# Two-batch hashed attention with two gated products behind it: a new order of the attention's work, a start with other buffers, and the first weights converted one pair later

## The chip, the cores and the metric

The kernel runs on one core of one Trainium2 chip. The metric is the device time of one execution in microseconds (us), the median of three runs. A core has five engines with queues of their own: TensorE (PE; PEld is its weight load), VectorE (DVE), ScalarE (ACT), GpSimd (POOL) and SyncE (SP, which here only issues DMAs). Each works through its own list in order and waits at semaphores for the others.

## The reference

Attention over 2 batches of 8 heads with 768 positions of width 64, where a query may only look at keys of its own hash bucket, then two products through wider layers:

```python
q_bits = (np.einsum('bhsd,dk->bhsk', q, proj) > 0)      # 6 bits a position; k likewise
mask = q_bucket[:, :, :, None] == k_bucket[:, :, None, :]
scores = np.where(mask, scale * q @ k.T, -1e9)
attn = softmax(scores); x = (attn @ v)                  # 1536 rows of 512
x = (sigmoid(x @ w_gate) * (x @ w_val)) @ w_out         # 512 -> 1536 -> 512
h = x @ w_in                                            # 512 -> 2048
g = h where h >= 1, 0 where h <= -1, else (h + 1) ** 2 / 4
out = g @ w_out2                                        # 2048 -> 512
```

The five weight matrices come as 64-bit floats. A chunk of 128 x 512 is brought to 32 bits on the chip and split into a high and a low part, and a product of two such numbers takes three matmuls.

## The kernel before

**Pairs and units.** Two heads make a pair; there are 8 pairs. A pair has 12 units, a unit being 128 queries of one head against all 768 keys. For each unit: `QK` (4 matmuls: two add the mask by one-hot rows, two the scores), `MAX` (the row maximum, DVE, L305), `EXP` (ACT, L309). Two units of the two heads make a Flip: `T` transposes 4 blocks of 128 x 128 (PE, L329), `HI` writes them to half precision (ACT, L338), `LO` the remainder (DVE, L341); there are 18 of each in a pair. `PV` multiplies with v (PE, L380) in three parts for each third of the queries, `EV` (L387) scales the result into X; `ST`, `RB`, `R` and `RS` turn the sums of the exponentials into row factors. The PSUM tiles are few: two `sc` tiles for scores, two `pt` tiles for transposes, one `mm`, one `pv`.

**Preparation of the next pair** (class `Prep`) runs beside this. q and k are loaded (`load_qk`), scaled and split into U (high) and W (low) by `scale`, `top`, `rest` on GpSimd. `z` projects them on PE, `bits` takes signs on ACT, `xp` multiplies the signs with the table of codes, `H` makes the one-hot rows of it on ACT. `copy` moves half tiles across partitions by DMA on SP's queue: N<-U, U<-W, W<-N, N<-H, H<-U.

**What sets the order.** A table `AT` (L463) gives each kind of operation its place, counted in units from the start of its pair; a place may be negative or beyond 12, and then lies in the pair before or behind. All operations of all pairs are sorted by place (L598) and issued in that order, so the table alone sets how each engine's list reads. Nothing is scheduled at run time.

**The start.** The first pair has no pair before it. Its split runs on ACT and DVE (`UW`), its tiles are moved by `first_moves` and `swap` on SP (L246, L259), its products with the codes are held in two `sc` tiles (`xp`, L452 to L460). 12 matmuls on a tile of zeros run ahead (`idle`, L434). The first chunk of `w_gate` is loaded between the q and k of pair 0 and of pair 1 (L432), that of `w_val` behind v (L450). Both are converted by `first_weights`, whose steps stand at places -1.25 to 4.75 of pair 0 (L590); its tiles are taken from the tags PT and P of the attention.

**The end of the attention and the rest.** `gv(0)` (L597), the first half of the first gate and value products, stands behind the last transposes; its DVE product (L154) is issued with it. Then come the gate and value products, `out1`, and `mlp2`, which ends with one evacuation and one DMA for each 128 rows (L678).

Of the kernel before, what the change touches and what calls it, by code (L numbers as in the profile page):

```python
# [27 lines left out]
def lsh_attention_glu_act(ctx, tc, qt, kt, v, proj, w_gate, w_val, w_out1, w_in2, w_out2, ident_d, code_d, out):  # L28
# [115 lines left out]

    X = {}

    def gate_val_n(b, n, ws, hr, bank, sgt, nm):
# [6 lines left out]
        nc.vector.scalar_tensor_tensor(out=hr[:, n * HN:(n + 1) * HN], in0=sg, scalar=1.0, in1=pv, op0=ALU.add, op1=ALU.mult)  # L154

    with ExitStack() as actx:
        ap = actx.enter_context(tc.tile_pool(name="attn", bufs=2))
# [22 lines left out]
        class Prep:  # L180
# [67 lines left out]
            def first_copies(self):
                tU, tW, tH, tN, tB = self.t4[0]
                for dst, src in ((tN[O], tU[O]), (tH[E], tU[E])):  # L250
                    nc.scalar.activation(out=dst, in_=f(src), func=AF.Copy)
# [145 lines left out]
        with tc.manual_schedule():  # L397
            ws0, wraw = [], []

            def load_w(w, t):  # L400
# [50 lines left out]
            pp.bits()
            hold = []  # L452
            for j in range(2):
                pp.xp(j)
                hold.append(pp.x_ps)
            for dst, r in ((2, O), (3, E)):
                pp.x_ps = hold[0]
                pp.Hot(0, pp.t4[0][dst], r)
                pp.x_ps = hold[1]
                pp.Hot_k(pp.t4[1][dst], r)  # L460
            pp.done()
            next(fw)
            AT = {  # L463
                "QK": (-2.69, -2.15, -0.16, -0.04, 1.61, 3.54, 3.80, 5.03, 6.14, 7.33, 8.42, 8.60),
                "MAX": (-2.19, -0.38, 0.24, 1.43, 3.32, 4.18, 4.48, 5.61, 6.44, 8.18, 8.87, 9.62),
                "EXP": (-0.83, -0.27, 0.55, 2.99, 3.75, 4.59, 5.42, 6.75, 8.09, 8.26, 8.91, 9.66),
# [13 lines left out]
                "TOP": (-3.20, -1.20),  # L480
                "RST": (-2.90, -0.90),
                "V2": (1.65,),
                "V3": (2.65,),
                "V4": (4.65,),
                "RB": (3.00, 8.00, 10.83),
                "VR": (9.72,),
                "VT": (11.80,),
# [39 lines left out]
            def split_x(b, c):  # L527
# [10 lines left out]
            for q in range(NQ):
                us = un[UP * q:UP * q + UP]
# [224 lines left out]
```

## Time and profile before

| what | us |
|---|---|
| median of 3 runs (lowest, highest) | 830.96 (830.45, 831.16) |
| profiled execution | 829.85 |
| its span (first to last instruction) | 827.8 |
| busy: PE | 805.3 |
| busy: DVE | 550.4 |
| busy: ACT | 457.3 |
| busy: POOL | 117.8 |

The profile is one execution. A busy time is the union of an engine's instructions; of PE the ends are modelled, so that a busy PE can still lose time between matmuls. Instructions of one engine overlap a little: one may start before the one ahead has ended, so a step is read from start to start. Attention takes the first 259 us, the products the rest.

### The profile page before, as it was taken

To read this page: it belongs to the slowest core of one execution; us is meant where nothing else is said; L and a number is where in the kernel's file an instruction comes from. 1 tells how busy PE (TensorE), PEld (TensorE's weight loads), DVE (VectorE), ACT (ScalarE), POOL (GpSimd) and SP (SyncE) were. 2 spreads that over 40 slices of the span, in tenths; PEclk is the share of its full clock that TensorE was granted. 3 is DMA by queue.
4 is the path that set the end of the run, shared out by engine and by line. 5 is a ranking of instruction groups with operands and counts; after the bars stand their busy time and mean duration, and the time that the engine had idled before them with its cause. 6 is when DMAs were issued, how large, how long until landed. Compare 5 with 4: busy or idle time off the path is not lost.

```text
span 827.8 us, 13043 instructions
## 1 busy us (share of the span) xinstructions
PE 805.3 (97%) x5084; PEld 735.8 (89%) x5084; DVE 550.4 (66%) x976; ACT 457.3 (55%) x870; POOL 117.8 (14%) x103
## 2 busy tenths in 40 slices
PE   6799999999998999999999999999999999999997
PEld 4688888888778999999999999999899999999996
DVE  4999898989993754345489767999944435344443
ACT  4788888888882422223233435557655455545453
POOL 4263445435073000000000000000000000000000
PEclk7999999999999999999999999999999999999999
DMA  7443544443201413211245320453200001000001
GB/s 230 115 95 99 134 107 96 125 125 68 59 1 62 144 51 94 60 51 52 89 165 179 96 82 27 152 175 126 81 1 1 1 0 77 1 1 1 1 0 77
DMA packets 39581, 64.21 MB, mean 78 GB/s; under 512 B 5316, under 2 KB 27972, under 8 KB 39520
## 3 DMA queue, kind: packets, MB, share of 16 engines
q1 hardware_dynamic: 39168, 63.20, 26.4%
q8 instruction: 40, 0.66, 0.3%
q14 instruction: 21, 0.17, 0.1%
q0 software_dynamic: 48, 0.11, 0.0%
q10 hardware_dynamic: 304, 0.07, 0.0%
HBM read 45.27 MB, written 3.15 MB: 58 GB/s over the span
## 4 chain that ended last, share of the span: by engine, by line
PE 80%; DVE 10%; DMA 6%; ACT 2%; issue 2%; SPq 0%; DVEq 0%; ACTq 0%
PE sc L297 7%; PE pt L329 7%; PE O L380 6%; PE o L676 5%; PE o L677 5%; PE o L675 5%; PE p L128 4%; PE p L130 4%; PE p L129 4%; PE pg L130 4%; PE pv L129 4%; PE pv L130 4%; PE pg L128 4%; PE pv L128 4%; PE pg L129 4%; PE y L129 2%
## 5 line engine op out<-in xcount | busy, mean ns | idle before, releaser
L341 DVE SCALAR_TENSOR_TENSOR PT<-pt,PT 128x512 f16<-128x512 f32 x144 | 96.4, 685 | 10.7 <-ACT PT L338 7.5
L305 DVE TENSOR_REDUCE st<-sc 128x1 f32<-128x768 f32 x96 | 90.9, 947 | 9.4 <-PE sc L297 9.3
L338 ACT ACTIVATE PT<-pt 128x512 f16<-128x512 f32 x144 | 82.1, 596 | 22.6 <-PE pt L329 21.4
L309 ACT ACTIVATE P<-sc,st 128x768 f32<-128x768 f32 x96 | 86.9, 905 | 13.5 <-DVE st L305 13.2
L329 PE MATMUL pt<-ident,P 128*128 128x128 f32 x576 | 83.2, 279 | 4.5 <-DVE PT L341 3.8
L128 PE MATMUL p<-yh,wh_i 128*128 128x384 f32 x256 | 86.1, 336 | 0.4 <-DVE yl L632 0.3
L130 PE MATMUL p<-yh,wl_i 128*128 128x384 f32 x256 | 85.9, 336 | 0.0
L129 PE MATMUL p<-yl,wh_i 128*128 128x384 f32 x256 | 85.7, 335 | 0.0
L329 PEld LDWEIGHTS pt<-ident,P 128*128 128x128 f32 x576 | 66.2, 142 | 18.5 <-DVE PT L341 11.5
L677 PE MATMUL o<-wh_o,gl 128*128 128x512 f32 x192 | 75.3, 392 | 0.0
L676 PE MATMUL o<-wl_o,gh 128*128 128x512 f32 x192 | 75.2, 392 | 0.0
L675 PE MATMUL o<-wh_o,gh 128*128 128x512 f32 x192 | 74.7, 389 | 0.0
L659 DVE SCALAR_TENSOR_TENSOR g<-p,t 128x384 f32<-128x384 f32 x64 | 35.5, 555 | 48.3 <-ACT t L657 48.3
L154 DVE SCALAR_TENSOR_TENSOR h<-sg,pv 128x384 f32<-128x384 f32 x48 | 26.4, 550 | 53.9 <-PE pv L130 53.9
L660 ACT ACTIVATE gh<-g 128x384 fp32r<-128x384 f32 x64 | 33.6, 525 | 43.7 <-DVE g L659 43.5
L152 ACT ACTIVATE sg<-pg 128x384 f32<-128x384 f32 x48 | 23.4, 487 | 62.1 <-PE pg L130 61.6
L656 ACT ACTIVATE t<-p,cst 128x384 f32<-128x384 f32 x64 | 36.6, 573 | 36.8 <-PE p L130 36.8
L380 PE MATMUL O<-PT,vh 128*64 128x256 f16 x576 | 54.9, 278 | 1.7 <-DVE xr L387 1.7
L661 DVE TENSOR_TENSOR gl<-g,gh 128x384 fp32r<-128x384 f32 x64 | 35.7, 558 | 31.5 <-ACT gh L660 31.5
L128 PEld LDWEIGHTS p<-yh,wh_i 128*128 128x128 f32 x256 | 48.1, 188 | 2.4 <-DVE g L659 0.7
L129 PEld LDWEIGHTS p<-yl,wh_i 128*128 128x128 f32 x256 | 48.1, 188 | 1.1
L118 DVE TENSOR_TENSOR wl_o<-w_o,wh_o 128x512 fp32r<-128x512 f32 x56 | 38.6, 689 | 14.7 <-ACT wh_o L117 14.7
(258 smaller groups left out, 2015.6 us busy)
## 6 DMA issues: line engine op xcount, KB each, us to landing
wr_o<-in_moe_w_out_dram SPq DMA_DIRECT2D x28, 512.0 KB, 3.5
wr_i<-in_moe_w_in_dram SPq DMA_DIRECT2D x16, 512.0 KB, 3.8
wr_g<-in_moe_w_gate_dram SPq DMA_DIRECT2D x12, 512.0 KB, 3.6
wr_v<-in_moe_w_val_dram SPq DMA_DIRECT2D x12, 512.0 KB, 4.0
n<-in_qt_dram SPq DMA_DIRECT2D x8, 384.0 KB, 3.7
n<-in_kt_dram SPq DMA_DIRECT2D x8, 384.0 KB, 4.3
U<-W SPq DMA_DIRECT2D x16, 192.0 KB, 2.5
vr<-in_v_dram SPq DMA_DIRECT2D x8, 384.0 KB, 3.5
```

The source lines that it names most:

```text
L128: nc.tensor.matmul(ps, lhsT=wh, rhs=rh, start=first, stop=False)
L129: nc.tensor.matmul(ps, lhsT=wh, rhs=rl, start=False, stop=False)
L130: nc.tensor.matmul(ps, lhsT=wl, rhs=rh, start=False, stop=last)
L305: nc.vector.tensor_reduce(out=self.st[:, 0, self.c:self.c + 1], in_=self.sc[:, :, 0:HN], op=ALU.max, axis=AX.XY, negate=True)
L309: nc.scalar.activation(out=self.P, in_=self.sc[:, :, 0:HN], func=AF.Exp, bias=self.st[:, 0, self.c:self.c + 1], scale=1.0, accum_out=self. ...
L329: nc.tensor.transpose(self.ps[m][:, j, :], un[2 * self.n + e].P[:, a, c:c + 128], ident)
L338: nc.scalar.activation(out=self.part(0, m), in_=self.ps[m], func=AF.Copy, scale=PSCALE)
L341: nc.vector.scalar_tensor_tensor(out=self.part(1, m), in0=self.ps[m], scalar=PSCALE, in1=self.part(0, m), op0=ALU.mult, op1=ALU.subtract)
L380: nc.tensor.matmul(O_ps[r, 0:GN], lhsT=vv[m][:, e, i * D:(i + 1) * D], rhs=PT[:, l, e * NI + i, :], start=(s == 0), stop=(s == len(steps) ...
L675: nc.tensor.matmul(oacc[i], lhsT=gh[:, ts], rhs=wh, start=(fc == 0), stop=False)
L676: nc.tensor.matmul(oacc[i], lhsT=gh[:, ts], rhs=wl, start=False, stop=False)
L677: nc.tensor.matmul(oacc[i], lhsT=gl[:, ts], rhs=wh, start=False, stop=(fc == F2 - 1))
```

## The change

The table `AT` is replaced by another; its entries for GpSimd (SCL, TOP, RST, V2 to V4, RB) are now numbers of their own, too. Two lines of it:

```diff
-                "QK": (-2.69, -2.15, -0.16, -0.04, 1.61, 3.54, 3.80, 5.03, 6.14, 7.33, 8.42, 8.60),
+                "QK": (-1.70, 0.05, 0.37, 1.03, 1.87, 2.98, 4.26, 5.03, 5.80, 8.96, 9.44, 7.84),
-                "SCL": (-3.80,),
+                "SCL": (-2.94,),
```

The start, the first weights, the held product and the last rows:

```diff
-        nc.scalar.dma_start(proj_sb[E], proj)
-        nc.scalar.dma_start(proj_sb[O], proj)
+        nc.scalar.dma_start(proj_sb, proj)
...
-                raw = ap.tile([128, 2 * S], I64, tag="PT", bufs=3, name=f"wr_{t}_0")[:, 0:512]
+                raw = ap.tile([128, 512], I64, tag="wr", name=f"wr_{t}_0")
...
-                        wt = ap.tile([128, S], U32, tag="P", bufs=7, name=f"w_{t}_0")[:, 0:512]
+                        wt = ap.tile([128, 512], U32, tag="wt", name=f"w_{t}_0")
...
-            load_w(w_gate, "g")
             load_qk(*seq[1], nc.sync)
             idle = sc_tile("idle")
-            for i in range(12):
+            for i in range(26):
...
+            pp.first_copy(nc.gpsimd.tensor_copy, 0)
             p1.scale()
...
-            pp.first_copies()
+            pp.first_copy(nc.scalar.copy, 1)
             pp.z(0, 12)
             for j in range(2):
                 pp.swap(j)
+            pp.bits()
+            xq = sc_tile("xq")
+            xk = [pA.tile([128, 512], F32, tag="pt", bufs=PTB, name=f"xk_{n}")[:, 0:HN] for n in range(2)]
+            for j in range(2):
+                for a in range(2):
+                    nc.tensor.matmul(xk[a] if j else xq[:, a, 0:HN], lhsT=code[:, a, j, :], rhs=bt, start=True, stop=True)
...
+            pp.rest_copies()
+            pp.done()
             load_v(*seq[0], nc.sync)
+            load_w(w_gate, "g")
             load_w(w_val, "v")
...
-            for i in range(7):
-                at(i - 1.25, 0, 0, next, fw, None)
+            for i in range(10):
+                at(2.0 * i, 0, 1, next, fw, None)
...
+            at(max(AT["LO"] + AT["EV"][1:2]) + 0.01, 0, last, lambda: late.pop()())
...
+            if b == B - 1 and i == NI - 1:
+                for eng, h, fn in ((nc.sync, 0, nc.vector.tensor_copy), (nc.scalar, 1, nc.scalar.copy)):
+                    cs = slice(h * DM // 2, (h + 1) * DM // 2)
+                    fn(ob[:, 1, cs], oacc[i][:, cs])
+                    eng.dma_start(rows[:, i, cs], ob[:, 1, cs])
+                continue
```

`proj` is now laid twice under itself by the host, so that one DMA fills both halves. The two copies of B (`rest_copies`) stand behind the one-hot rows instead of ahead of `z`. `first_weights` has ten steps instead of eight; the first ran ahead of the table and now all ten stand in it, in pair 1 and the first half of pair 2. `gate_val_n` takes a list and, for `gv(0)`, puts its DVE product there, to be issued behind the last LO and the second EV.

Three places, as the built programs list them. First SP's list from the loads of pair 0 on; n are q and k, wr_g and wr_v the raw weight chunks, B, N, H, U and W tiles of the pair. Before:

```order
L166 DMA n_0_0_78<-in_kt_dram 128x768
L402 DMA wr_g_96<-in_moe_w_gate_dram 128x4x128
L166 DMA n_0_1_98<-in_qt_dram 128x768
L166 DMA n_0_1_100<-in_kt_dram 128x768
L246 DMA B_133<-U_0_0_115 64x768
L246 DMA N_0_0_122<-U_0_0_119 64x768
L246 DMA B_137<-U_0_0_119 64x768
L246 DMA H_0_0_121<-U_0_0_119 64x768
L259 DMA U_0_0_115<-W_0_0_116 64x768
L259 DMA U_0_0_119<-W_0_0_120 64x768
L172 DMA vr_0_165<-in_v_dram 128x2x384
L402 DMA wr_v_167<-in_moe_w_val_dram 128x4x128
```

The same stretch of SP's list in the changed program:

```order
L171 DMA n_0_0_78<-in_kt_dram 128x768
L171 DMA n_0_1_94<-in_qt_dram 128x768
L171 DMA n_0_1_96<-in_kt_dram 128x768
L251 DMA B_143<-U_0_0_125 64x768
L251 DMA N_0_0_132<-U_0_0_129 64x768
L251 DMA B_148<-U_0_0_129 64x768
L251 DMA H_0_0_131<-U_0_0_129 64x768
L266 DMA U_0_0_125<-W_0_0_126 64x768
L266 DMA U_0_0_129<-W_0_0_130 64x768
L177 DMA vr_0_190<-in_v_dram 128x2x384
L406 DMA wr_g_192<-in_moe_w_gate_dram 128x4x128
L406 DMA wr_v_194<-in_moe_w_val_dram 128x4x128
```

The load of the first gate chunk has moved from ahead of pair 1's q and k to behind v.

Second, DVE's list from the last third of pair 0 to the first MAX of pair 1 (xr is EV's result, vm the maximum over v, sc the scores). Before:

```order
L315 RECIPROCAL st_0_0_2_291<-st_0_0_2_291 128x4
L341 SCALAR_TENSOR_TENSOR PT_0_1_360<-pt_0_411,PT_0_1_360 128x4x128
L305 TENSOR_REDUCE st_0_0_4_405<-sc_0_1_4_417 128x1
L341 SCALAR_TENSOR_TENSOR PT_0_1_360<-pt_2_439,PT_0_1_360 128x4x128
L305 TENSOR_REDUCE st_0_0_4_405<-sc_0_0_5_469 128x1
L341 SCALAR_TENSOR_TENSOR PT_0_1_360<-pt_1_452,PT_0_1_360 128x4x128
L387 SCALAR_TENSOR_TENSOR xr_0_510<-O_0_0_375,rs_0_1_1_393 128x256
L305 TENSOR_REDUCE st_0_0_4_405<-sc_0_1_5_486 128x1
L341 SCALAR_TENSOR_TENSOR PT_0_2_517<-pt_0_498,PT_0_2_517 128x4x128
L341 SCALAR_TENSOR_TENSOR PT_0_2_517<-pt_1_505,PT_0_2_517 128x4x128
L349 TENSOR_REDUCE vm_1_538<-vr_1_391 128x1
L305 TENSOR_REDUCE st_1_0_0_545<-sc_1_0_0_512 128x1
```

The same stretch of DVE's list in the changed program:

```order
L345 SCALAR_TENSOR_TENSOR PT_0_1_328<-pt_2_371,PT_0_1_328 128x4x128
L309 TENSOR_REDUCE st_0_0_4_395<-sc_0_1_5_390 128x1
L345 SCALAR_TENSOR_TENSOR PT_0_1_328<-pt_0_403,PT_0_1_328 128x4x128
L353 TENSOR_REDUCE vm_1_454<-vr_1_368 128x1
L345 SCALAR_TENSOR_TENSOR PT_0_1_328<-pt_1_413,PT_0_1_328 128x4x128
L309 TENSOR_REDUCE st_0_0_4_395<-sc_0_1_4_418 128x1
L345 SCALAR_TENSOR_TENSOR PT_0_2_469<-pt_0_464,PT_0_2_469 128x4x128
L309 TENSOR_REDUCE st_0_0_4_395<-sc_0_0_5_458 128x1
L345 SCALAR_TENSOR_TENSOR PT_0_1_328<-pt_2_475,PT_0_1_328 128x4x128
L391 SCALAR_TENSOR_TENSOR xr_0_519<-O_0_0_423,rs_0_1_1_398 128x256
L309 TENSOR_REDUCE st_1_0_0_528<-sc_1_0_0_511 128x1
```

The last unit's MAX now comes ahead of the two before it, and the first MAX of pair 1 stands behind EV with one LO fewer ahead of it.

Third, DVE's list at the end of the attention, around the product of `gv(0)` (L154, h<-sg,pv). Before:

```order
L341 SCALAR_TENSOR_TENSOR PT_3_2_3526<-pt_0_3561,PT_3_2_3526 128x4x128
L341 SCALAR_TENSOR_TENSOR PT_3_2_3526<-pt_1_3609,PT_3_2_3526 128x4x128
L154 SCALAR_TENSOR_TENSOR h_0_3623<-sg_0_0_3637,pv_0_0_3639 128x384
L341 SCALAR_TENSOR_TENSOR PT_3_2_3526<-pt_2_3616,PT_3_2_3526 128x4x128
L387 SCALAR_TENSOR_TENSOR xr_3_3524<-O_3_1_3528,rs_3_1_3_3550 128x256
L387 SCALAR_TENSOR_TENSOR xr_3_3524<-O_3_2_3655,rs_3_1_5_3671 128x256
```

The same stretch of DVE's list in the changed program:

```order
L345 SCALAR_TENSOR_TENSOR PT_3_2_3500<-pt_1_3584,PT_3_2_3500 128x4x128
L316 TENSOR_SCALAR st_3_0_4_3439<-st_3_0_4_3439,vm_3_3093 128x4
L319 RECIPROCAL st_3_0_4_3439<-st_3_0_4_3439 128x4
L345 SCALAR_TENSOR_TENSOR PT_3_2_3500<-pt_2_3604,PT_3_2_3500 128x4x128
L391 SCALAR_TENSOR_TENSOR xr_3_3546<-O_3_1_3565,rs_3_1_3_3553 128x256
L154 SCALAR_TENSOR_TENSOR h_0_3625<-sg_0_0_3639,pv_0_0_3641 128x384
L391 SCALAR_TENSOR_TENSOR xr_3_3546<-O_3_2_3676,rs_3_1_5_3660 128x256
```

The product has moved behind the last LO and the second EV.

## Rows read from the trace of the kernel before

**Rows 1.** Stretch, length, busy us of PE, PEld, DVE, ACT, POOL; PE clock, DMA, GB/s
```profile
0.00:17.40 17.40, 10.29 (x33) 5.85 (x34) 7.01 (x17) 7.58 (x9) 8.58 (x11) 0.81 0.79 232
17.40:48.80 31.40, 26.64 (x175) 21.48 (x175) 29.19 (x48) 23.03 (x48) 11.36 (x10) 0.89 0.45 118
...
77.30:105.80 28.50, 28.39 (x252) 23.64 (x251) 25.55 (x45) 24.50 (x51) 13.18 (x11) 1.00 0.45 112
...
219.80:259.00 39.20, 36.05 (x334) 30.04 (x334) 28.97 (x53) 25.27 (x52) 24.41 (x21) 1.00 0.01 1
...
822.60:827.80 5.20, 0.01 (x1) 0.00 (x0) 0.06 (x1) 0.60 (x1) 0.00 (x0) 0.88 0.53 206
```
**Rows 2.** Timeline: first MAX of pairs 0, 1 and 7 (start, duration, engine, line)
```profile
17.43 0.96 DVE L305 TENSOR_REDUCE st<-sc 128x1 f32<-128x768 f32 x1 [2.74 <-PE sc L297]
...
48.77 0.95 DVE L305 TENSOR_REDUCE st<-sc 128x1 f32<-128x768 f32 x1
...
219.77 0.95 DVE L305 TENSOR_REDUCE st<-sc 128x1 f32<-128x768 f32 x1
```
**Rows 3.** Timeline of the start: loads landing, the swaps, the first scores
```profile
4.40 0.84 ACT L200 ACTIVATE U<-n 128x768 fp32r<-128x768 f32 x1 [0.53 <-DMA n<-in_qt_dram]
...
5.62 0.84 ACT L200 ACTIVATE U<-n 128x768 fp32r<-128x768 f32 x1 [0.37 <-DMA n<-in_kt_dram]
...
12.67 1.30 SPq L259 DMA_DIRECT2D U<-W  x2
...
16.41 0.98 PE L297 MATMUL sc<-U,U 128*128 128x384 f32 x2 [1.11 <-DMA U<-W]
```
**Rows 4.** Waits of SP's queue: total us, times, longest
```profile
SPq L259 <- DMA B<-U: 4.4, 2, 4.2
```
**Rows 5.** Groups by line: two of the conversion's steps (busy us, mean ns)
```profile
L102 DVE SCALAR_TENSOR_TENSOR w_g<-wr_g,w_g 128x512 uint32<-128x512 uint32 x12 | 8.3, 691 | 0.4
...
L99 DVE TENSOR_SCALAR w_g<-w_g 128x512 uint32<-128x512 uint32 x12 | 5.1, 421 | 0.1
```
**Rows 6.** Timeline: a conversion step beside GpSimd in pair 0
```profile
26.00 2.33 POOL L361 TENSOR_SCALAR vr<-vr,vm 128x768 f32<-128x768 f32 x1 [8.33 <-DMA vm<-vrow]
...
26.30 1.01 DVE L99 TENSOR_SCALAR w_v<-w_v 128x512 uint32<-128x512 uint32 x1
```
**Rows 7.** Timeline of pair 3: steps of PE and DVE
```profile
118.00 1.04 PE L329 MATMUL pt<-ident,P 128*128 128x128 f32 x8
...
118.79 0.59 PE L297 MATMUL sc<-H,H 128*128 128x384 f32 x2
...
119.27 1.29 DVE L341 SCALAR_TENSOR_TENSOR PT<-pt,PT 128x512 f16<-128x512 f32 x2
...
119.57 0.34 PE L228 MATMUL xp<-bt,code 128*128 128x384 bf16 x1
...
120.47 0.95 DVE L305 TENSOR_REDUCE st<-sc 128x1 f32<-128x768 f32 x1
...
121.34 0.41 DVE L387 SCALAR_TENSOR_TENSOR xr<-O,rs 128x256 f32<-128x256 f32 x1
...
129.40 0.85 PE L380 MATMUL O<-PT,vh 128*64 128x256 f16 x12
```
**Rows 8.** Timeline of pair 3: last H, its second DMA, next pair's first product
```profile
126.21 0.59 ACT L235 ACTIVATE H<-xp,cst 128x384 fp32r<-128x384 f32 x1
...
129.34 0.46 SPq L275 DMA_DIRECT2D H<-U  x1
...
131.99 0.41 PE L297 MATMUL sc<-H,H 128*128 128x384 f32 x1
```
**Rows 9.** Timeline of the hand-over: PE behind the second EV
```profile
256.24 0.30 PE L380 MATMUL O<-PT,vh 128*64 128x256 f16 x2 [1.74 <-DVE xr L387]
```
**Rows 10.** Timeline of the last rows: evacuation and two DMA issues
```profile
822.65 0.60 ACT L683 ACTIVATE ob<-o 128x512 f32<-128x512 f32 x1 [0.76 <-PE o L677]
822.69 1.08 SPq L685 DMA_DIRECT2D out_dram<-ob  x2
```

More of the change, by code (lines that the diff above doesn't have):

```diff
@@ L74, in constants @@
             nc.vector.tensor_tensor(out=pz[r, 1, cs], in0=proj_sb[r], in1=pz[r, 0, cs].bitcast(F32), op=ALU.subtract)
-        nc.vector.tensor_copy(code[0:ZR], code_f)
     def f(ap):
@@ L145, in lsh_attention_glu_act, with gate_val_n @@
     X = {}
-    def gate_val_n(b, n, ws, hr, bank, sgt, nm):
+    def gate_val_n(b, n, ws, hr, bank, sgt, nm, late=None):
         (gh, gl), (vh, vl) = ws
@@ L153, in gate_val_n, with product @@
         pv = proj_chunk(bank(f"pv_{nm}"), vh, vl, xs, n)
-        nc.vector.scalar_tensor_tensor(out=hr[:, n * HN:(n + 1) * HN], in0=sg, scalar=1.0, in1=pv, op0=ALU.add, op1=ALU.mult)
+        def product():
+            nc.vector.scalar_tensor_tensor(out=hr[:, n * HN:(n + 1) * HN], in0=sg, scalar=1.0, in1=pv, op0=ALU.add, op1=ALU.mult)
+        if late is None:
+            product()
+        else:
+            late.append(product)
     with ExitStack() as actx:
@@ L246, in first_moves, with first_copy, rest_copies @@
                     nc.sync.dma_start(f(dst), f(src))
[L248 to L251, printed above, removed]
+            def first_copy(self, fn, m):
+                tU, tW, tH, tN = self.t4[0][0:4]
+                dst, r = ((tN, O), (tH, E))[m]
+                fn(out=dst[r], in_=f(tU[r]))
+            def rest_copies(self):
                 for j in range(2):
@@ L259, in swap @@
                 nc.sync.dma_start(f(tU[s0]), f(tW[s1]))
-            def Hot_k(self, dst, r):
-                nc.vector.tensor_scalar(out=v2(dst)[r], in0=self.x_ps[r], scalar1=float(NB) - 1.0, scalar2=1.0, op0=ALU.is_ge, op1=ALU.subtract)
             def H(self, j, n=None):
@@ L423, in first_weights @@
                     w_low(wt, low)
+                    yield
                     w_sign(wt, high)
@@ L431, in lsh_attention_glu_act @@
             constants()
-            load_w(w_gate, "g")
             load_qk(*seq[1], nc.sync)
             idle = sc_tile("idle")
-            for i in range(12):
+            for i in range(26):
                 nc.tensor.matmul(idle[:, 0, 0:HN], lhsT=bt[:, 0:128], rhs=bt, start=True, stop=True)
             pp, p1 = Prep(*seq[0]), Prep(*seq[1])
-            for j in range(2):
-                pp.UW(j)
-                pp.first_moves(j)
+            pp.UW(0)
+            pp.first_moves(0)
+            nc.vector.tensor_copy(code[0:ZR], code_f)
+            pp.UW(1)
+            pp.first_moves(1)
+            pp.first_copy(nc.gpsimd.tensor_copy, 0)
             p1.scale()
@@ L448, in lsh_attention_glu_act @@
                 pp.swap(j)
+            pp.bits()
[4 more added lines that the diff above has]
+                    nc.tensor.matmul(xk[a] if j else xq[:, a, 0:HN], lhsT=code[:, a, j, :], rhs=bt, start=True, stop=True)
+            for dst, r in ((2, O), (3, E)):
+                pp.x_ps = xq[:, :, 0:HN]
+                pp.Hot(0, pp.t4[0][dst], r)
+                for n in range(2):
+                    nc.vector.tensor_scalar(out=pp.t4[1][dst][r, n * HN:(n + 1) * HN], in0=xk[n][r], scalar1=float(NB) - 1.0, scalar2=1.0, op0=ALU.is_ge, op1=ALU.subtract)
@@ L449, in lsh_attention_glu_act @@
+            pp.rest_copies()
+            pp.done()
             load_v(*seq[0], nc.sync)
+            load_w(w_gate, "g")
             load_w(w_val, "v")
[L451 to L460, printed above, removed]
@@ L461, in lsh_attention_glu_act @@
-            pp.done()
-            next(fw)
-            AT = {
-                "QK": (-2.69, -2.15, -0.16, -0.04, 1.61, 3.54, 3.80, 5.03, 6.14, 7.33, 8.42, 8.60),
-                "MAX": (-2.19, -0.38, 0.24, 1.43, 3.32, 4.18, 4.48, 5.61, 6.44, 8.18, 8.87, 9.62),
-                "EXP": (-0.83, -0.27, 0.55, 2.99, 3.75, 4.59, 5.42, 6.75, 8.09, 8.26, 8.91, 9.66),
[9 rows of a table removed]
-                "BITS": (1.52,),
-                "XP": (2.12, 3.89, 4.91, 7.01),
-                "H": (3.68, 4.88, 5.53, 7.69),
-                "SCL": (-3.80,),
[L480 to L487, printed above, removed]
+            AT = {
+                "QK": (-1.70, 0.05, 0.37, 1.03, 1.87, 2.98, 4.26, 5.03, 5.80, 8.96, 9.44, 7.84),
+                "MAX": (-0.86, 0.21, 0.88, 1.91, 2.70, 4.35, 4.73, 5.39, 7.85, 9.79, 9.89, 9.06),
+                "EXP": (0.22, 0.67, 1.17, 2.60, 2.83, 4.40, 4.86, 7.05, 8.14, 9.79, 11.21, 9.27),
[9 rows of a table added]
+                "BITS": (3.03,),
+                "XP": (3.74, 4.91, 5.72, 7.78),
+                "H": (4.54, 5.60, 7.69, 8.77),
+                "SCL": (-2.94,),
+                "TOP": (-1.71, -2.70),
+                "RST": (-1.54, 1.43),
+                "V2": (6.89,),
+                "V3": (6.91,),
+                "V4": (8.71,),
+                "RB": (4.94, 9.36, 13.82),
+                "VR": (9.39,),
+                "VT": (12.02,),
@@ L531, in split_x @@
                 X[b, c] = hi, lo
+            late = []
             def gv(n):
@@ L535, in gv @@
                     HR[0, 0] = htile("h0_0")
-                gate_val_n(0, n, ws0, HR[0, 0], lambda nm: sc_tile(nm)[:, 0], lambda nm: ap.tile([128, HN], F32, tag="P", bufs=7, name=nm), f"0_0_{n}")
+                gate_val_n(0, n, ws0, HR[0, 0], lambda nm: sc_tile(nm)[:, 0], lambda nm: ap.tile([128, HN], F32, tag="P", bufs=7, name=nm), f"0_0_{n}", late if n == 0 else None)
             for q in range(NQ):
@@ L752 @@
     heads = {"qt": qt.reshape(b, h // 2, 2 * d, s), "kt": kt[:, :, ::-1].reshape(b, h // 2, 2 * d, s)}
-    named = {n: _np.ascontiguousarray(a) for n, a in (heads | {n: inputs[n] for n in _INS} | _tables()).items()}
+    named = {n: _np.ascontiguousarray(a) for n, a in (heads | {n: inputs[n] for n in _INS} | {"proj": _np.tile(inputs["proj"], (2, 1))} | _tables()).items()}
     named = {n: a.view(_np.int64) if a.dtype == _np.float64 else a for n, a in named.items()}
```

18 rows, old and new, of the table AT are left out of this document.

## The prediction

> **What bounds the kernel now.** I read the busy times by stretch first [rows 1]. The products behind the attention are not shown there because nothing in them changes but the last rows; what can change lies in the start, the eight pairs, the hand-over and the last 5 us. In a middle pair PE is busy 28.39 of 28.50 us, DVE 25.55, ACT 24.50, POOL 13.18 [rows 1]. That looks like a pure PE bound, but PE's ends are modelled, so I read steps from start to start [rows 7]: eight transposes 0.79 (118.00 to 118.79), the four matmuls of a unit 0.78 (118.79 to 119.57), a part of PV at most 0.85. A pair has 12 units, 9 groups of eight transposes and 9 parts of PV: 9.4 + 7.1 + 7.7 = 24.2 us; 12 matmuls of z, 4 with the codes and 6 of R at no more than 0.78 / 4 = 0.195 add 4.3, in all 28.5 at most. These steps hold PE's changes from one kind to the next, so a pair is bound by PE together with the waits that the order puts between; DVE has 2.95 us free in each pair. Then the first MAX of the pairs [rows 2]: pair 0 takes 48.77 - 17.43 = 31.34 us, pairs 1 to 6 take (219.77 - 48.77) / 6 = 28.50 each.
>
> **The change part by part**, as a difference to the profiled execution (829.85 us: span 827.8 and 2.05 around it). The median of the three runs, 830.96, stands 1.11 above it; I add the sum to the median.
>
> *Start.* The first reduce waits for scores whose second half waits for the DMA U<-W (16.41, [rows 3]); U<-W was issued at 12.67 because SP waited for B<-U, 4.2 us once [rows 4]. All these DMAs go through one queue behind the loads. q lands at 4.40, k, of the same 384 KB, at 5.62 [rows 3]: 1.22 us each, so the 512 KB of the gate chunk take about 1.6. They now stand behind v, so B<-U, U<-W and the scores come that much earlier. I take -1.7; bounds -1.2, if the one-hot rows become the late ones, and -2.3. The single load of proj, the 14 further matmuls on zeros, the copies moved to GpSimd and behind the one-hot rows, the products with the codes in pt tiles: all lie under that wait for U<-W and are taken at nothing. Without that cover the dearest is the pair of copies of B, 2 of at most 0.95 (as long as a MAX, [rows 7]), or 1.9.
>
> *Pair 0.* DVE is busy 29.19 of 31.4 us [rows 1] and holds the conversion: for each of two chunks two steps of 0.42 and three of 0.69 [rows 5], in all 5.8. Without it DVE has 23.4 us left, so it no longer holds the pair; what is late next is the chain from transposes to LO and back to PE, as in a later pair. I take the length of a later pair in the new order (28.1, below): -3.2. Bounds: -5.3 (26, DVE's 23.4 and the 2.6 that the first units take to fill) and -1.3.
>
> *Pairs 1 to 6, the new places.* The same operations in another order; no row shows the new waits. Below, DVE's 25.55 is the floor, above, I allow 29.5 (the chain of H, below). By the steps PE needs nearly all of the 28.5, and that row is the nearest, so I take little: 28.1, or 6 x -0.4 = -2.4. Bounds -17 and +6.
>
> *The conversion in pairs 1 and 2.* Six of its ten steps fall into pair 1, four into pair 2. DVE gets 2 x 0.42 + 2 x 0.69, then 0.69 + 2 x 0.42 = 3.75 in pair 1 and 2.07 in pair 2; with 25.55 that is 29.3 and 27.6. Against 28.1 only 1.2 us sticks out, so that is the lower bound. The upper one is all 5.8 with two more stretches like the one of pair 0, where a step of 0.42 took 1.01 while GpSimd worked on v [rows 6]: 7.0. Each step stands in DVE's list ahead of a LO or a MAX that PE or ACT waits for, so it is not free where DVE is free on the mean; I take +3.0. ACT's four steps are short and ACT has 4 us free. The gate chunk has landed long before; its own tiles make no one wait.
>
> The Trainium skill (SBUF — State Buffer, "Who interferes with whom") says that a DVE instruction with two SBUF inputs and a GpSimd instruction that reads SBUF exclude each other for a whole instruction. The 1.01 beside GpSimd agrees in kind, for a step with one tensor input. By that rule, with GpSimd busy 13.18 of 28.5, an estimate is 10 steps x 0.46 x 0.59 = 2.7 us, and the conversion would cost 5.7 instead of 3.0.
>
> *Where the pair is cut.* The first MAX of a pair has one LO fewer ahead of it, so the last pair has one more behind it: two LO take 120.47 - 119.27 = 1.20 [rows 7], hence +0.6.
>
> *Hand-over.* The product of `gv(0)` needs PE's value matmuls and was ahead of the last LO and of the second EV on DVE; PE then waited 1.74 us for EV to free the one pv bank [rows 9]. Now LO, and PV behind it, do not wait for the product; left is the EV itself, 0.41 [rows 7], and its two hand-overs, about 0.7. So -1.0; bounds -1.3 and 0. The product is queued last, and only the next gate product needs its bank.
>
> *Last rows.* The last evacuation, 0.60 on ACT, and the second of two issues (1.08 for both, [rows 10]) become two halves on two engines and two queues: -0.5, bounds -0.9 and 0.
>
> Sum: -1.7 - 3.2 - 2.4 + 3.0 + 0.6 - 1.0 - 0.5 = -5.2: 824.65 in the profiled execution, 825.8 for the median.
>
> **The rivals.**
> *A: the new places take out PE's waits,* a pair of 27.0. For it: PE's steps are upper bounds and DVE and ACT are far from full. Against it: PE is busy to 0.1 us. Seven pairs by 1.1 give -7.7, the conversion sticks out by 1.0 more: -11.9, 819.1.
> *B: the places are no better than the old,* 28.5: seven pairs by 0.4 back, -2.4, 828.6. For it: PE's sum of 28.5. Against: nothing that the rows show.
> *C: B, and the conversion is paid in full* (7.0 instead of 3.0): +1.6, 832.6; what pair 0 gives up comes back in pairs 1 and 2. For it: the row of 1.01.
> *D, slower: the one-hot chain becomes the wait at each pair's start.* The last H starts at 126.21, ends 0.59 later, N<-H goes, H<-U is issued at 129.34 when N<-H has landed, 2.5 us on; with as much again H lands near 131.9, and the next pair's first product starts at 131.99 [rows 8]. With 0.78 for the unit its MAX is ready 6.6 us behind the start of H. Until then DVE lives on its list: before, by the order shown, 6 LO, 3 MAX, EV and the maximum over v (taken as a MAX, 0.95), with 0.60, 0.87, 0.41 [rows 7] 7.6 us, so the chain is hidden; in the new list, from the last unit's MAX on, 3 MAX, 4 LO, EV and the maximum, 6.4. So 0.2 already sticks out, and each DMA that lands 0.5 later adds as much, twice in a chain. With a pair of 29.5, seven pairs cost 9.8 more and the conversion 1.5 less (DVE then has room): +3.1, 834.1. It decides from a pair of 28.9 on, where the seven pairs eat the whole gain.
>
> **How the numbers follow.** Chances: forecast 0.42, A 0.15, B 0.20, C 0.11, D 0.12. A measurement of this kernel tells about 0.2%, 1.7 us, from no change. Faster by more: all of A, most of the forecast and of B, 0.70. Within 1.7 us: the rest of these and most of C, 0.15. Slower: D and the rest of C, 0.15. The forecast's own range is 822 to 829. Taking in A's near side and C leaves out the far side of A and most of D: 817 to 833.
>
> **What would show it.** Right: the first MAX near 15.7; the second pair's near 44; pairs 3 to 6 near 28.1 apart; pairs 1 and 2 together about 3 us longer than two of these; PE's wait for EV near 0.7; nothing waits for H<-U beyond 0.2 us. Wrong: pairs 3 to 6 below 27.5 (A) or above 28.9 with PE waiting for the DMA H<-U (D); pairs 1 and 2 together 7 us longer (C); a start that waits for the one-hot rows.

## The result, and the profile after

The changed kernel takes 838.76 us (median of 4 runs, 836.99 to 840.51), the kernel before 830.71 beside it (830.36 to 831.16): a ratio of 1.0097, 95% interval 1.0075 to 1.0119. It is 8 us slower; the forecast was 825.8, range 817 to 833. The profiled execution took 836.99, with a span of 835.2 against 827.8.

Busy times by stretch, for the stretches of [rows 1] and for pair 1 (same columns: stretch, length, busy us of PE, PEld, DVE, ACT, POOL; PE clock, DMA share, GB/s):
```profile
0.00:16.00 16.00, 11.23 (x48) 6.34 (x48) 8.67 (x20) 6.06 (x7) 10.74 (x12) 1.00 0.81 242
16.00:44.20 28.20, 24.67 (x156) 20.10 (x157) 23.92 (x37) 20.67 (x44) 12.64 (x10) 0.88 0.57 144
44.20:75.90 31.70, 29.42 (x256) 24.20 (x255) 30.57 (x51) 26.32 (x56) 13.39 (x11) 1.00 0.41 101
104.90:134.00 29.10, 28.48 (x252) 23.87 (x251) 27.00 (x46) 24.25 (x52) 13.10 (x11) 1.00 0.43 109
221.30:267.70 46.40, 39.24 (x351) 32.44 (x349) 29.71 (x53) 25.70 (x53) 24.23 (x21) 0.96 0.01 1
830.30:835.20 4.90, 0.06 (x1) 0.00 (x0) 0.53 (x2) 0.37 (x1) 0.00 (x0) 1.00 0.59 223
```
In a middle pair PE works as long as before (28.48 against 28.39) and the pair is 0.6 longer; DVE, with the same operations, is busy 27.00 instead of 25.55. The stretch from the last pair's first MAX to the last EV grew from 39.2 to 46.0.

The first MAX of pairs 0, 1, 3, 4 and 7, in the timeline of DVE, beside [rows 2]:
```profile
15.98 0.94 DVE L309 TENSOR_REDUCE st<-sc 128x1 f32<-128x768 f32 x1
...
44.23 0.96 DVE L309 TENSOR_REDUCE st<-sc 128x1 f32<-128x768 f32 x1 [0.22 <-PE sc L301]
...
104.88 0.95 DVE L309 TENSOR_REDUCE st<-sc 128x1 f32<-128x768 f32 x1
...
133.95 0.96 DVE L309 TENSOR_REDUCE st<-sc 128x1 f32<-128x768 f32 x1 [0.22 <-PE sc L301]
...
221.31 0.96 DVE L309 TENSOR_REDUCE st<-sc 128x1 f32<-128x768 f32 x1 [0.28 <-PE sc L301]
```
The last EV (the third of the last pair), before and after, and the first MAX of pair 3 before:
```profile
258.99 0.42 DVE L387 SCALAR_TENSOR_TENSOR xr<-O,rs 128x256 f32<-128x256 f32 x1 [2.90 <-PE O L380]
```
```profile
267.35 0.42 DVE L391 SCALAR_TENSOR_TENSOR xr<-O,rs 128x256 f32<-128x256 f32 x1 [1.86 <-PE O L384]
```
```profile
105.84 0.95 DVE L305 TENSOR_REDUCE st<-sc 128x1 f32<-128x768 f32 x1
```
From these, the difference of the two spans by stretch:

| stretch | before | after | difference | forecast |
|---|---|---|---|---|
| start, to the first MAX | 17.43 | 15.98 | -1.45 | -1.7 |
| pair 0 | 31.34 | 28.25 | -3.09 | -3.2 |
| pairs 1 and 2 | 57.07 | 60.65 | +3.58 | +2.2 (conversion +3.0, places -0.8) |
| pairs 3 to 6 | 113.93 | 116.43 | +2.50 | -1.6 |
| last pair, to the last EV | 39.22 | 46.04 | +6.82 | -0.4 (cut +0.6, hand-over -1.0) |
| the rest | 568.78 | 567.86 | -0.92 | -0.5 |

The sum is +7.44, as by the spans. Two rows of the table are the miss: the steady pairs, with the wrong sign, and the last pair, where nearly the whole loss lies.

**The last pair.** GpSimd's steps on v and its first split of X before, in the timeline (start, duration, engine, line):
```profile
226.66 2.21 POOL L361 TENSOR_SCALAR vr<-vr,vm 128x768 f32<-128x768 f32 x1 [5.03 <-DMA vm<-vrow]
...
230.49 1.66 POOL L368 TENSOR_TENSOR vl<-vr,vh 128x768 f16<-128x768 f32 x1
232.10 0.83 POOL L529 CAST x_0h<-xr 128x768 fp32r<-128x768 f32 x1
```
And after:
```profile
235.64 0.83 POOL L538 CAST x_0h<-xr 128x768 fp32r<-128x768 f32 x1
236.55 1.81 POOL L539 TENSOR_TENSOR x_0l<-xr,x_0h 128x768 fp32r<-128x768 f32 x1
238.31 0.83 POOL L538 CAST x_1h<-xr 128x768 fp32r<-128x768 f32 x1
239.22 1.82 POOL L539 TENSOR_TENSOR x_1l<-xr,x_1h 128x768 fp32r<-128x768 f32 x1
241.02 2.20 POOL L365 TENSOR_SCALAR vr<-vr,vm 128x768 f32<-128x768 f32 x1
243.28 0.82 POOL L368 CAST vh<-vr 128x768 f16<-128x768 f32 x1
244.05 0.83 POOL L538 CAST x_2h<-xr 128x768 fp32r<-128x768 f32 x1
244.96 1.80 POOL L539 TENSOR_TENSOR x_2l<-xr,x_2h 128x768 fp32r<-128x768 f32 x1
246.72 1.64 POOL L372 TENSOR_TENSOR vl<-vr,vh 128x768 f16<-128x768 f32 x1
```
And PE and the next MAX in the same stretch:
```profile
244.16 0.30 PE L384 MATMUL O<-PT,vh 128*64 128x256 f16 x2 [1.34 <-POOL vh L368]
248.41 0.43 PE L384 MATMUL O<-PT,vl 128*64 128x256 f16 x2 [3.95 <-POOL vl L372]
...
249.62 1.01 PE L301 MATMUL sc<-H,H 128*128 128x384 f32 x2
...
253.15 0.95 DVE L309 TENSOR_REDUCE st<-sc 128x1 f32<-128x768 f32 x1
```
The splits of X keep their places 5.0 + 1.7c in the last pair; the steps on v went from 1.65, 2.65 and 4.65 to 6.89, 6.91 and 8.71. So two splits now run ahead of the scaling of v and a third between vh and vl; PE, which has PV at the head of its list, waits 1.34 and 3.95 us. Behind that, after 4 us in which it did nothing, PE runs at half speed for most of a stretch (columns as above): the granted clock is 0.56 in it and 0.50, the 1.2 GHz level, in its first part.
```profile
248.40:251.90 3.50, 3.49 (x20) 2.92 (x21) 0.00 (x0) 0.00 (x0) 3.42 (x4) 0.56 0.00 0
```
```profile
248.40:250.00 1.60, 1.59 (x11) 1.12 (x12) 0.00 (x0) 0.00 (x0) 1.52 (x3) 0.50 0.00 0
```

**The steady pairs.** DVE and GpSimd in pair 4 (the step L316 of 128x4 is ST):
```profile
151.03 1.29 DVE L345 SCALAR_TENSOR_TENSOR PT<-pt,PT 128x512 f16<-128x512 f32 x2
152.40 1.62 DVE L316 TENSOR_SCALAR st<-st,vm 128x4 f32<-128x4 f32 x1
154.06 0.18 DVE L319 RECIPROCAL st<-st 128x4 f32<-128x4 f32 x1
```
```profile
149.18 2.20 POOL L365 TENSOR_SCALAR vr<-vr,vm 128x768 f32<-128x768 f32 x1
151.44 0.82 POOL L368 CAST vh<-vr 128x768 f16<-128x768 f32 x1
152.35 1.64 POOL L372 TENSOR_TENSOR vl<-vr,vh 128x768 f16<-128x768 f32 x1
```
The step ST, four numbers to a partition, starts 0.05 us behind GpSimd's subtraction for vl and ends when that ends: 1.62 us, where it takes 0.22 elsewhere (the median of its 24). It is held, that is, kept from running until its neighbour is done. So it is in each of pairs 3 to 6, and it is the 1.4 us by which DVE's busy time grew. The two LO at 151.03, with one input in PSUM, took their usual 1.29 beside the scaling and the cast. The Trainium skill (SBUF — State Buffer, "Who interferes with whom") says that a one-input operation of DVE such as `tensor_scalar`, in its fast mode with both ends in SBUF, and an instruction of GpSimd lock each other out for a whole instruction; the 1.62 agrees.

**Start, hand-over, last rows**, beside [rows 3], [rows 9] and [rows 10]:
```profile
13.30 2.76 DVE L261 CAST B<-W 64x768 fp32r<-64x768 f32 x2
...
22.29 0.27 DVE L358 TENSOR_REDUCE vrow<-vrow 1x1 f32<-1x128 f32 x1 [1.65 <-DMA vrow<-vm]
```
```profile
13.64 2.01 POOL L215 TENSOR_TENSOR W<-n,U 128x768 fp32r<-128x768 f32 x1
```
```profile
265.08 0.30 PE L384 MATMUL O<-PT,vh 128*64 128x256 f16 x2 [0.52 <-DVE xr L391]
...
830.40 0.42 DVE L694 COPY ob<-o 128x256 f32<-128x256 f32 x1
...
830.86 0.37 ACT L694 COPY ob<-o 128x256 f32<-128x256 f32 x1 [1.22 <-DVE ob L694]
```
The first MAX now stands behind the two copies of B, of which the second is held until GpSimd's subtraction of W ends at 15.65. At the fourth MAX, 23.09 for 23.80, half of the 1.4 us is gone again: ahead of it DVE waits for vrow. PE's wait for the EV fell from 1.74 to 0.52. The two halves of the last rows do not run side by side: ACT's starts when DVE's has ended.

### The profile page after: what moved, and what is told of

Its sections match the earlier page's. It is cut to its first block, busy times and chain, and to the rows that moved or that the text cites. A ratio compares the mean times of both kernels' runs of the same rounds, so it can differ in the third digit from the quotient of the medians.

```text
span 835.2 us, 13047 instructions
## 1 busy us (share of the span) xinstructions
PE 808.9 (97%) x5098; PEld 738.6 (88%) x5098; DVE 559.4 (67%) x979; ACT 454.0 (54%) x869; POOL 119.6 (14%) x104
## 4 chain that ended last, share of the span: by engine, by line
PE 81%; DVE 7%; ACT 6%; DMA 3%; POOL 1%; issue 1%; SPq 0%; ACTq 0%; POOLq 0%; DVEq 0%
PE p L126 5%; PE p L128 5%; PE p L127 5%; PE o L688 5%; PE o L689 5%; PE o L687 5%; PE sc L301 5%; PE pt L333 4%; PE pg L128 4%; PE pg L126 4%; PE pv L126 4%; PE pv L127 4%; PE pv L128 4%; PE pg L127 4%; PE y L127 4%; PE y L126 4%
## 5 line engine op out<-in xcount | busy, mean ns | idle before, releaser
L333 PE MATMUL pt<-ident,P 128*128 128x128 f32 x576 | 80.9, 277 | 5.6 <-DVE PT L345 4.9
L671 DVE SCALAR_TENSOR_TENSOR g<-p,t 128x384 f32<-128x384 f32 x64 | 35.5, 555 | 48.3 <-ACT t L669 48.3
L154 DVE SCALAR_TENSOR_TENSOR h<-sg,pv 128x384 f32<-128x384 f32 x48 | 26.4, 551 | 50.5 <-PE pv L128 50.5
```

Source lines behind the costliest of these rows:

```text
L333: nc.tensor.transpose(self.ps[m][:, j, :], un[2 * self.n + e].P[:, a, c:c + 128], ident)
```

## The experiments

Four theories are tried: (1) GpSimd's splits ahead of v make the last pair; (2) the last pair is long because more PV stands behind the cut; (3) the steady pairs lose by the held ST; (4) they lose by something else in the order, as the chain of H. Each run was timed beside the kernel before on its chip; ratios are to that. The length of a pair is the distance from its first MAX to the next pair's, and all lengths and waits are from the profiled execution. Runs 1 to 3 change the changed kernel, run 4 the kernel before.

**1. The splits ahead of v.**
```
-                at(5.0 + 1.7 * c, 0, last, split_x, 0, c)
+                at(1.85 + 0.01 * c, 0, last, split_x, 0, c)
```
Expected: 

> The changed kernel; only the four splits of X of batch 0 in the last pair stand earlier in GpSimd's list, ahead of the steps on v instead of among them at 5.0 + 1.7c. Theory 1 (in the last pair vh and vl came late because GpSimd had the splits in front of them): the last EV comes 40 us behind the last pair's first MAX instead of 46.1, no wait of PE for vh or vl over 1 us; 838.8 becomes 832 to 833. Theory 2 (the last pair is long because the new places put more PV behind the cut): within 1 us of 838.8. Either way pairs 3 to 6 stay 29.1.


Measured: 831.87, ratio 1.0014 (1.0004 to 1.0023); the last EV 40.3 behind the last pair's first MAX; no wait of PE for vh or vl; pairs 3 to 6 at 29.0 to 29.1. Theory 1 holds and 2 falls: moving four splits gives back 6.9 us.

**2. The steps on v early.**
```
-                "V2": (6.89,), "V3": (6.91,), "V4": (8.71,),
+                "V2": (2.00,), "V3": (2.02,), "V4": (2.04,),
```
Expected: 

> The changed kernel; only the three steps of GpSimd on v stand at 2.00 to 2.04 of their pair instead of 6.89 to 8.71, so they come ahead of the splits of the last pair and end before the second sum of a pair. Theory 1 and theory 3 (the 0.6 us that each steady pair lost comes from the step ST that takes 1.62 instead of 0.22 us beside GpSimd's subtraction for vl): last EV 40 behind the last pair's first MAX, no ST over 0.5 us, pairs 3 to 6 at 28.5: 828 to 830. Theory 1 with theory 4 (the 0.6 comes from elsewhere in the new order, as the chain of H): pairs 3 to 6 stay at 29.1, 832 to 833.


Measured: 826.93, ratio 0.9958 (0.9943 to 0.9973). The last pair took 39.1, and in pairs 3 to 6 no ST over 0.25 was left (DVE busy 25.6 to 25.7). That is what theories 1 and 3 say, and the time is below the 828 to 830 expected. The edit moves three steps at once; that the ST is what it frees is read from the trace. But pairs 3 to 6 took 28.30, 28.85, 28.79 and 28.21. In all four DVE's maximum over v waits for its load, 1.2 us in the two longer ones and 0.6 in the others:
```profile
155.60 0.95 DVE L353 TENSOR_REDUCE vm<-vr 128x1 f32<-128x768 f32 x1 [1.21 <-DMA vr<-in_v_dram]
```
So a new wait came up where the hold went: with DVE 1.4 us earlier, the load (issued at 5.9 of a pair) is late. In the changed kernel the hold covered this wait: it shows once, 0.6 us, in pair 2, the one pair but the last without an ST of 1 us or more.

**3. The old places, all else changed** (the lines of the table are left out).
```
-            AT = { new }
+            AT = { old }
```
Expected: 

> The changed kernel with the old table of places (GpSimd's steps on v at 1.65 to 4.65, as before); all else of the change stays. If the table alone made the loss: first MAX at 16.0, pairs 3 to 6 at 28.5, last EV 39 to 40 behind the last pair's first MAX, pairs 1 and 2 together 2.5 to 3 over two of these; 830.7 - 1.4 - 3.1 + 2.6 - 1.0 = 827.8. If something else of the change (the own tiles, the order of loads, the conversion) made it: pairs at 29.1 or a last pair of 46 remain, 832 or more.


Measured: 827.23, ratio 0.9959 (0.9942 to 0.9977). Pairs 4 to 6 at 28.5 and the last pair 37.0: with the old places the loss is gone, and the rest of the change gains 3.1. In parts it differs from what was expected: first MAX at 14.2 (the two copies of B took 1.80 there), pair 0 30.5, and pairs 1 and 2 5.9 over two of 28.5, not 2.6. At the end of pair 0 PE waited 2.77 for H<-U. The profiled execution took 829.01, the longest of six, so these parts add up to more than the median.

**4. The new places alone, in the kernel before.** The edit is the reverse of run 3's.
Expected: 

> The kernel before with the new table of places and nothing else of the change. If the table alone made the loss: pairs 3 to 6 at 29.1, last EV 46 behind the last pair's first MAX, 830.7 + 6 x 0.6 + 6.5 = 841. If the table needs the rest of the change to lose: 831.


Measured: 838.50, ratio 1.0096 (1.0081 to 1.0111). Pairs 1 to 6 near 29.1, the last EV 46.8 behind the last pair's first MAX, PE's waits for vh and vl 1.4 and 4.0. The loss is there without the rest. The sum came out 2.5 lower than expected; 1.6 of it is pair 0, which fell to 29.7 with the conversion still in it. Pair 3 here has no held ST, and it is no shorter (29.26): the wait for the load of v stands in its place.
```profile
130.49 0.95 DVE L349 TENSOR_REDUCE vm<-vr 128x1 f32<-128x768 f32 x1 [1.50 <-DMA vr<-in_v_dram]
```

**5. The load of v earlier**, on top of 2.
```
-                    at(5.9, 0, q, load_v, *seq[q + 1])
+                    at(2.9, 0, q, load_v, *seq[q + 1])
```
Expected: 

> The kernel of the run with GpSimd's steps on v at 2.00 to 2.04, and the load of the next pair's v issued at 2.9 of a pair instead of 5.9. Theory: there the pairs of 28.8 are those in which DVE's maximum over v waits up to 1.2 us for that load; then all of pairs 3 to 6 take 28.2 to 28.3, and the time is 2 us below that run's 826.9, near 825. Rival: the maximum only stands in a gap that is there anyway, and pairs go on at 28.3 and 28.8: 826.9.


Measured: 823.42, ratio 0.9907 (0.9891 to 0.9924). This is more than was expected: pairs 3 to 6 take 27.76, and PE shows no gap in them (two pairs, columns as above):
```profile
103.70:131.40 27.70, 27.70 (x252) 23.76 (x251) 25.55 (x44) 23.56 (x49) 12.95 (x11) 1.00 0.44 115
131.40:159.20 27.80, 27.80 (x253) 23.84 (x251) 25.66 (x46) 24.00 (x51) 13.16 (x12) 1.00 0.44 115
```
So the order of PE, DVE and ACT in the new table is better by 0.74 a pair than the old one; the places of the steps on v and of one load hid it. Theory 4 falls with this, but for that load: its place was not changed, and it is late only in the new order.

**6. The copies of B ahead of z**, on top of 5.
```
             pp.first_copy(nc.scalar.copy, 1)
+            pp.rest_copies()
...
-            pp.rest_copies()
             pp.done()
```
Expected: 

> As the run with the load of v at 2.9, and the two copies of B of the first pair stand on DVE ahead of z's products, where DVE waits 3.2 us for the products with the codes, instead of behind the one-hot rows. Theory: these copies (2.76 us, the second held until GpSimd's subtraction of W ended) are what the first MAX waits for at 16.0; it comes at 14.4 to 14.6, behind U<-W, 1.5 us less in all: near 823.5. Rival: U<-W and the PE behind it are as late: the first MAX stays within 0.3 us of 16.0, no change against the run beside it.


Measured: 823.69, ratio 0.9918 (0.9897 to 0.9940): no change. The first MAX came at 14.9, in run 5 at 14.4 without this edit. Where the start ends varies between executions: with the same start it came at 16.0 to 16.2 in the changed kernel and in runs 1, 2 and 12; in run 5 both copies had started ahead of GpSimd's subtraction of W. In runs 5 and 6 the fourth MAX stands at 23.4 to 23.7, as in the changed kernel (23.1): in run 5 the wait for vrow grew to
```profile
22.58 0.27 DVE L358 TENSOR_REDUCE vrow<-vrow 1x1 f32<-1x128 f32 x1 [3.56 <-DMA vrow<-vm]
```
A gain at the start is eaten there, so this run could not decide on B.

**7 and 8. The conversion in the last pair, and in pair 0**, on top of 6.
```
-                at(2.0 * i, 0, 1, next, fw, None)
+                at(1.1 * i, 0, NQ - 1, next, fw, None)     # in run 7
+                at(1.0 + 1.0 * i, 0, 0, next, fw, None)    # in run 8
```
Expected, run 7: 

> As the run with the copies of B moved, and the ten steps of the conversion stand in the last pair, 1.1 apart from 0, instead of in pairs 1 and 2. Theory: pair 1 is 2.7 us longer than its neighbours only for the conversion, and in the last pair DVE has 9 us free: pair 1 falls to 28.3, the last pair grows by 1 at most, the time falls by 2, near 821.5. Rival: the last pair pays what pair 1 paid, 2.7: no change.


Expected, run 8: 

> As the run with the copies of B moved, and the ten steps of the conversion stand in pair 0, 1.0 apart from 1.0 on, instead of in pairs 1 and 2. Pair 0 took 29.70 with the conversion (the kernel before with the new places) and 28.25 without (the changed kernel): by that it costs 1.5 there and pair 1 gives 2.7 back, so 1.2 us less, near 822.3. Rival: in pair 0 it costs as much as in pairs 1 and 2: no change.


Measured: 828.71, ratio 0.9970 (0.9960 to 0.9980), and 825.41, ratio 0.9931 (0.9916 to 0.9946): both worse than 6, by 5.0 and 1.7. Neither the theory nor the rival held in either. Pairs 1 and 2 gave 4.4 and 4.8 back, but the last pair took 48.3 instead of 39.1, and pair 0 36.9 instead of 28.7. In the last pair the steps meet GpSimd's splits; six of the ten on DVE are held, 5.1 us in all:
```profile
230.29 1.86 POOL L539 TENSOR_TENSOR x_1l<-xr,x_1h 128x768 fp32r<-128x768 f32 x1
230.52 1.91 DVE L97 TENSOR_SCALAR w_v<-w_v 128x512 uint32<-128x512 uint32 x1
...
233.19 1.81 POOL L539 TENSOR_TENSOR x_2l<-xr,x_2h 128x768 fp32r<-128x768 f32 x1
233.55 2.00 DVE L100 SCALAR_TENSOR_TENSOR w_v<-wr_v,w_v 128x512 uint32<-128x512 uint32 x1
```
(They take 0.43 and 0.68 where GpSimd rests.) PE waited 3.1 us for the LO behind the first of these. DVE's free time in the mean, 9.5 us in that pair, was no room for them. In pair 0 two steps were held, 1.0 us in all. There DVE had waited 4.79 for vrow before the first of its steps, and nine of its ten, in two bunches, then stood ahead of LO and MAX. PE waited 4.55 for LO up to 27.10, and its granted clock was 0.50 from 26.2 to 32.9 and again from 39.9 to 43.2 (0.81 over the pair, 0.90 in run 6):
```profile
26.20:32.90 6.70, 5.80 (x22) 5.43 (x23) 5.92 (x9) 4.39 (x11) 4.99 (x3) 0.50 0.62 165
```
What of the 8 us is the bunches, the wait for vrow and the clock was not tried.

**9. The weight chunks loaded late**, on top of 6.
```
-            load_w(w_gate, "g")
-            load_w(w_val, "v")
...
+            at(9.45, 0, 0, load_w, w_gate, "g")
+            at(9.46, 0, 0, load_w, w_val, "v")
```
Expected: 

> As the run with the copies of B moved, and the two chunks of weights are loaded at 9.45 of pair 0 instead of at the start. Theory: in pair 0 DVE's small steps on the maximum of v stand ahead of the fourth MAX and wait (1.65 us in the changed kernel, 3.56 with the early load of v) for the DMA vrow<-vm, which sits behind the two chunks and lands at 22.3 to 22.8 whatever the start was; without them it lands 3 us behind its issue, near 21, the fourth MAX comes near 21.3 instead of 23.7, and the time falls by 2 to 2.5, to 821.3. Rival: another wait of pair 0 takes its place (pt or N<-U): no change.


Measured: 822.91, ratio 0.9917 (0.9897 to 0.9937); 6 had 0.9918. In the trace the mechanism is as expected: no wait for vrow, the fourth MAX at 20.4, pair 0 26.1 instead of 28.7. But pairs 1 and 2 grew by 1.6: the conversion starts at the first place of pair 1, and its chunk, issued at 38.2, has not landed (ACT's wait in pair 1: total us, times, longest):
```profile
ACT w_g L93 <- DMA wr_g<-in_moe_w_gate_dram: 1.6, 1, 1.6
```
The timed runs spread over 3.3 us, and no gain in the time is shown: the wait for one load was turned into a wait for another.

**10 and 11. The conversion spread over pairs 1 to 5**, on top of 9, at places where GpSimd rests (10) and beside its steps (11).
```
-            for i in range(10):
-                at(2.0 * i, 0, 1, next, fw, None)
+            for q, d in ((1, 7.0), (1, 8.505), (2, 0.9), (2, 8.505), (3, 0.0), (3, 8.505), (4, 0.9), (4, 8.505), (5, 0.0), (5, 8.505)):
+                at(d, 0, q, next, fw, None)
```
(in 11 with 10.52 for 8.505 and 2.95 for 0.9)
Expected, run 10: 

> As the run with the late chunks, and the ten steps of the conversion spread over pairs 1 to 5, two to a pair, at 0 or 0.9 and at 7.0 or 8.505, where GpSimd rests. Theory: what the conversion cost in pairs 1 and 2 (4.5 us against pairs of 27.77) is DVE held up at single places, by GpSimd's instructions (1.28 for 0.68, 1.48 for 0.68) and by steps in a row ahead of a LO; spread, a pair of 27.77 with DVE busy 25.6 takes in 1.2 us, and pairs 1 to 5 stay under 28.1: 3 us less than the run beside it, near 818. Rival: PE has no slack at all and pays each step: 1.2 in each of five pairs, no change.


Expected, run 11: 

> As the spread conversion, but the steps that stood at 0.9 and 8.505 stand at 2.95 and 10.52, beside GpSimd's steps on v and its subtraction of W. By the rule of the Trainium skill (SBUF — State Buffer, Who interferes with whom) a step of DVE with both operands in SBUF is held until GpSimd's instruction ends: seven steps of 0.43 to 0.69 become 1.3 to 2 each, and pairs 1 to 5 grow by 0.7 to 1 each: 4 over the run at the free places, 822. Rival: only the count of steps at one place matters: as fast as that run.


Measured: 817.70, ratio 0.9854 (0.9838 to 0.9870), and 820.33, ratio 0.9888 (0.9871 to 0.9904). Run 10 is the fastest of all, 12.4 us below the kernel before and 5.2 below run 9; its pairs 1 to 5 sum to 141.2 against 144.9 there, none of its steps is held, and its conversion starts at 7.0 of pair 1, when the chunk has landed. The same step in run 10, and in run 11 with its neighbour on GpSimd:
```profile
74.84 0.67 DVE L100 SCALAR_TENSOR_TENSOR w_g<-wr_g,w_g 128x512 uint32<-128x512 uint32 x1
```
```profile
79.35 0.82 POOL L368 CAST vh<-vr 128x768 f16<-128x768 f32 x1
79.52 1.19 DVE L100 SCALAR_TENSOR_TENSOR w_g<-wr_g,w_g 128x512 uint32<-128x512 uint32 x1
```
In run 11 the six steps with two inputs took 1.02 to 1.19 instead of 0.67 to 0.69, and one of the others 0.58 instead of 0.42: DVE is held 2.5 us in all, and pairs 1 to 5 sum to 143.7, 2.5 more. A place beside GpSimd costs what it holds; it held less than was expected, so 2.5 instead of 4. Part of it shows as PE's wait, four times and 2.1 us in all, for an EV that stands behind a held step.

**12. The copies of B at their new place, chunks late**: run 9 without the edit of 6.
Expected: 

> As the run with the late chunks, but the copies of B stand behind the one-hot rows as in the changed kernel. Theory: with the wait for vrow<-vm gone the start counts again, and where a copy of B is held by GpSimd's subtraction the first MAX comes at 16 instead of 14.5: up to 1.5 us more than the run with B ahead. Rival: the copies hide behind U<-W: within 0.5 us of that run.


Measured: 823.51, ratio 0.9925 (0.9910 to 0.9939) against 0.9917 for run 9. In the trace the first MAX came at 16.0 against 14.1, and PE waited 1.6 for B; in the time the intervals overlap. The mechanism is seen, its worth in the time is open.

## Why the prediction was wrong

*The failed step is "Pairs 1 to 6, the new places", and with it "Where the pair is cut".* The first took -0.4 a pair from PE's sum and the row nearest to it. It treated the new places as an order of PE, DVE and ACT; the steps of GpSimd, which the table also moves, were not followed. By run 5 the order itself is worth -0.74, so the sign was right for what was looked at; a hold of 1.4 us by GpSimd's new place, and behind it a load that comes late, turned it into +0.6. The prediction had the rule and a row of a longer step beside GpSimd [rows 6], and used both only for the conversion. (That row by itself does not show a hold to the end: the step of 1.01 ended at 27.31, GpSimd's instruction at 28.33.)

*"Where the pair is cut"* counted one LO, +0.6. It has no term for GpSimd's list in that pair and gives no reason for this: there is no next pair to prepare there, but four splits, at places that did not move with those of v. That was to be had from the order before any run: three splits ahead of vl, 2.65 us each, and PE's PV behind it. It cost 5.3 us of waits and a stretch at half clock; run 1 gave 6.9 back. None of the rivals was this; D, the slower one, had another place, and it did not come: PE waits 0.7 in all for H<-U, at most 0.25 at a time. (The six LO that D counts before are those of the trace from 126.36 on; the list shown has five of them, and with five its 7.6 is 7.0, still more than 6.6.)

*Right in number, and in part by luck:* pair 0, -3.1 for -3.2. The sum took it for as long as a later pair of the new order, 28.1; the later pairs took 29.1 and pair 0 28.25. And what it names as the gain is the conversion that leaves DVE. With the old places that gave 0.9 (30.5 in run 3), and the new places with the conversion still in pair 0 gave 1.6 (29.7 in run 4). The conversion: pairs 1 and 2 came 2.4 over two of 29.1, for +3.0. But pair 2 has no held ST, which hides part of the cost: in runs 3, 5 and 6 it was 5.9, 4.8 and 4.5 over two of their later pairs, and the 5.7 by the rule, which the sum did not take, is nearer to these. Two of its steps were held in the changed kernel (1.28 and 1.46 for 0.68), and runs 7, 10 and 11 show that its size hangs on where it meets GpSimd.

*Right:* the hand-over, 0.52 for the 0.7 forecast. The start, -1.4 for -1.7; but the cover named there failed, since the copies of B came out from under the wait for U<-W, and the gate chunk that now stands behind v comes ahead of vrow, a wait that the sum did not have. The last rows: from the first evacuation of the last 128 rows to the end 4.8 instead of 5.1 [rows 10], 0.3 for 0.5. Of the -0.9 behind the last EV that leaves 0.6 which was not traced.

## What to carry to other kernels

When a table moves the steps of a helper engine, list what else is in that engine's queue in each kind of stretch, the last above all, and see whom PE meets at its head. Then lay the helper's instructions in time beside DVE's steps that have all operands in SBUF: here a step of 0.2 us was paid with what was left of its neighbour. And when a hold is taken away, look for the transfer that it covered.

## What the hardware showed that was not expected

- A step of four elements to a partition is held like a large one: 1.62 us for 0.22. The 96 MAX and 144 LO of the changed kernel, which read PSUM, took at most 0.96 and 0.69, beside the same GpSimd instructions too.
- A DMA of 0.5 KB (vrow, pair 0) landed 3.0 to 6.8 us behind its issue where the two loads of 512 KB had been issued 4.5 to 7.4 us ahead of it on SP (the changed kernel, runs 1 to 3 and 5 to 8), and within 2.1 with one of them or none (the kernel before, runs 4 and 9 to 12).
- After PE had waited 1.34 and 3.95 us, a part of PV, one unit and eight transposes ran at a granted clock of 0.56 in the mean; two products of 128x384 took 1.01 where they take 0.59 [rows 7].
